# A fused attention and expert kernel on one core: one more chunk of unit 2's first product ahead of unit 1's second, eight g buffers for five, and a table of shifts on the planner's due times

## The chip, the cores and the metric

The kernel runs on one core of one Trainium2 chip, in one launch. The metric is the device time of that core in microseconds. The kernel before has a median of 1087.2 us over three runs (1081.66 to 1087.91).

## The reference, cut to what matters

```python
# attention with decay: 8 batches x 8 heads, 576 positions, head size 64, all float32
cum = np.cumsum(np.log(np.clip(f, 0.0001, 1.0)), axis=-1)
scores = q @ k.T / 8 + cum[:, None] - cum[None, :]      # causal
attn = exp(scores - rowmax) / (rowsum + 1e-9)
x = (attn @ v)          # -> 4608 tokens x 512, heads side by side
# expert
h = x @ w_in            # 512 -> 2048
g = h * np.cos(h)
out = g @ w_out         # 2048 -> 512
```

w_in and w_out arrive as float64.

## The kernel before, in words

**Work.** A batch has four pairs of heads, `n` = 0 to 31 in all. For each pair the kernel loads q and k with the running sums of log f, forms the scores in PSUM (TensorE, "PE"), takes the row extremum (VectorE, "DVE", L692 or L853), the exponential (ScalarE, "ACT", L702 or L858), turns the weights round, multiplies them with v (L729 or L908) and leaves x as two float16 halves `xh` and `xl`. The first four pairs go through `attention32` (plain float32, turned on PE at L655); the others go through `attention`, whose weights are turned by a DMA transpose (L884). Pairs 0 to 3 hold their q and k in the ring `g` (`load32`, L619 to L627).

**The expert** is cut in units: two per batch, of 320 and 256 tokens, numbered `u` = 0 to 15 in the code (unit 1 and unit 2 of the title are `u` = 0 and `u` = 1). `gemm1(u, c)` (L924) makes chunk c of four of the first product: four groups of twelve matmuls (L938), each group into one tile of the PSUM ring `hp` (three tiles), each tile copied by ACT into the SBUF ring `h` (three buffers, L944). Then follow, for the chunk as a whole, two DVE operations into `r` (one buffer, L953 and L955), ACT's sine (L957), DVE's product with h (L959), ACT's float16 copy (L966) and the remainder on DVE or POOL (L967 or L968); the last two write the ring `g`. `gemm2(u, m)` (L971) reads the four g buffers of a unit: 48 matmuls (L984) into one `hp` tile, ACT's scaled copy (L990), a store.

**Weights.** Both matrices are read as pairs of 32-bit words and put together by three DVE operations per tile (L483, L487, L491), squared on ACT for a bound (L502) and split in two float16 halves by ACT (L512) and DVE (L519). Raw tiles of w_in pass through the ring `h`, those of w_out through the ring `g`.

**What sets the order.** Nothing is issued while the code runs through its loops: `op` only records operations with a cost, an engine and a priority `prio`, and their dependences. Rings are handed out in that recording order: buffer k of a ring waits for all users of buffer k minus the ring's size, and the first operation on a ring's buffer comes behind the first operation on the buffer before it. So in the recording order of `moe(u)` chunk 0 of unit u, the four `gemm2` of unit u-1 and chunks 1 to 3 of unit u take the `hp` tiles, and PE keeps to that order. In the first stretch the ring `g` is handed to the q and k of pairs 0 to 3 and to the sixteen raw tiles of w_out by turns: the second head of pair 1 stands five places behind the first head of pair 1.

`order` then plans: `rank` gives due times, `forward` runs a list schedule on modelled engines (at each step an engine takes, of what is ready, the operation with the earliest due time; a change of ACT's function table counts as `SWITCH` = 6 us of lateness), `backward` gives new due times from the end, and a second `forward` gives the order in which every engine's instructions are written. `forward` may also move an operation to its second engine (`alt`), and where PE would be idle in the first 200 us it writes filler matmuls on a constant tile (`pads`, L1050). Each engine runs its list in the order written; SP issues all DMAs from one list.

Of the kernel before, what the change touches and what calls it, by code (L numbers as in the profile page):

```python
# [40 lines left out]
POOLW = ()  # L41
SLQ, SLW, SLG = 1.0, 50.0, 0.0
LEAD = 2.5
HOLDV, HOLDW, HOLDR, HOLDX = 0.0, 0.0, 25.0, 18.0
NHP = 3
N32, NQ = 4, 8
ROUNDS = 2
AHEAD = 15
FILL, PAD = 200, 448
SWITCH = 6.0  # L50
TWO_PI = 2.0 * np.pi
NEG = -8.0e9
BUFS = dict(xs=1, stage=2, v2=2, vv=2, pt3=3, pt2=2, xh0=8, xl0=8, xh1=8, xl1=8, h=3, r=1, g=5, ot=1,
            pa2=1, pa1=3, hp=3, dg=1)


class Buf:
# [77 lines left out]
class Plan:  # L135
# [5 lines left out]
    def ring(self, name, make):  # L141
        old = self.rings.setdefault(name, [])
        b = Buf(make)
        if len(old) >= BUFS[name]:
            b.wait = old[len(old) - BUFS[name]]
        b.prev, b.name = old[-1] if old else None, name
# [86 lines left out]
    def order(self):  # L233
        self.rank()
        base = [(o.eng, o.cost, o.fn) for o in self.ops]
        for k in range(ROUNDS):
            if k:
                self.backward(end)
            for o, x in zip(self.ops, base):
                o.eng, o.cost, o.fn = x  # L240
            out, end = self.forward()
        return out

    def forward(self):

        free, avail, future, out, ends = {}, {}, [], [], {}
        for o in self.ops:
            free.setdefault(o.eng, 0.0)
            avail.setdefault(o.eng, [])
            o.n, o.ready = len(o.deps), o.hold  # L250
            if not o.n:
                heapq.heappush(future, (o.hold, o.id, o))
        t, dma_free, table, span = 0.0, 0.0, None, 0.0
        free["PE"] = PE0
        pe, port = Clock(), dict.fromkeys(SHARED, 0.0)
        while len(out) < len(self.ops):
            while future and future[0][0] <= t + 1e-9:
                _, _, o = heapq.heappop(future)
                if o.alt:
                    def done(e, c):  # L260
                        return max(t, free[e]) + c + sum(x.cost for x in avail[e] if x.due - x.first <= o.due - o.first)

                    if done(o.alt[0], o.alt[1]) <= done(o.eng, o.cost) + o.alt[3]:
                        o.eng, o.cost, o.fn = o.alt[:3]
                avail[o.eng].append(o)
            nxt = []
            for e, q in avail.items():
                if q and free[e] <= t + 1e-9:
                    o = min(q, key=lambda x: (x.due - x.first + (SWITCH if x.table not in (None, table) else 0.0), x.id))
                    q.remove(o)  # L270
                    out.append(o)
                    o.t = t
                    end = t + o.cost
                    if e == "PE":
                        o.pads = 0
                        if o.fill and t < FILL:
                            a = max([free[e]] + [x.end + 0.25 for x in o.bank])
                            if t - a > PADG:
                                o.pads = pe.pad(a, t - PADE)
                        end = pe.run(t, o.cost, o.moving)  # L280
                    if o.port and e in port:
                        x = port[SHARED[e]]
                        both = min(o.cost, max(0.0, x - t))
                        end += both
                        if both:
                            free[SHARED[e]] += both
                            port[SHARED[e]] += both
                        port[e] = end
                    if o.table not in (None, table):
                        table = o.table  # L290
                        end += T_TABLE
                    free[e] = end
                    if e == "SP":
                        dma_free = max(dma_free, t + min(o.cost, 0.625) + T_DMA0) + o.size / (DMA_BW if t > 10.0 else 0.6 * DMA_BW)
                        end = dma_free
                        if o.cost > 1.0:
                            free[e] = max(t + o.cost, end - 0.925)
                    span = max(span, end)
                    ends[o.id] = o.end = end
                    for s in o.succ:  # L300
                        s.ready = max(s.ready, end + (T_DMA1 if e == "SP" else LAT[e, s.eng]))
                        s.n -= 1
                        if not s.n:
                            heapq.heappush(future, (s.ready, s.id, s))
                if q:
                    nxt.append(free[e])
            if future:
                nxt.append(future[0][0])
            assert nxt or len(out) == len(self.ops), "operations wait for one another"
            t = max(t, min(nxt, default=t))  # L310
        self.span = span
        return out, ends
# [27 lines left out]
def fox_moe_kernel(ctx: ExitStack, tc: tile.TileContext, qkT, vp, fT, w1, w2, out):  # L340
    nc = tc.nc
# [59 lines left out]
    def ring(name, shape, dt, space=pool, tag=None):  # L401
        tag = tag or name
        return pl_.ring(tag, lambda: space.tile(shape, dt, name=tag, bufs=BUFS[tag]))

# [519 lines left out]
    def gemm1(u, c, pr):  # L924
        b, half = divmod(u, NU)
        w_ = UW[half]
        inv, a1, b1, o1 = ms[b]
        h = ring("h", [P, 4, UM], F32)
        for k in range(4):
            fs = slice(k * P, k * P + P)  # L930
            hp = ring("hp", [P, 512], F32, psum)

            def mm(hp=hp, fs=fs):
                n = 0
                for cb in range(NC):
                    xh, xl = X[b * NP + cb][half]
                    for w, x in ((0, xh), (1, xh), (0, xl)):
                        T.matmul(hp.get()[:, 0:w_], WS_[1][:, at(1, 4 * c + cb), w, fs], x.get(), start=(n == 0), stop=(n == 11))  # L938
                        n += 1

            xs = [z for cb in range(NC) for z in X[b * NP + cb][half]]
            op("PE", 12 * c_mm(w_), mm, reads=[*xs, *(WB[1, at(1, 4 * c + i)].part(j) for i in range(4) for j in range(3))], writes=[hp], prio=pr,
               fill=lambda hp=hp: hp.get()[:, 0:PAD])
            op("ACT", c_act(w_, True), lambda hp=hp, k=k: A.activation(  # L944
                h.get()[:, k, 0:w_], hp.get()[:, 0:w_], AF.Copy, scale=float(2.0 ** -24)), reads=[hp], writes=[h.part(k)], prio=pr)
        r = ring("r", [P, 4, UM], F32)
        hk = [h.part(k) for k in range(4)]
        N = 4 * w_

        def fl(x):  # L950
            return x.get()[:, :, 0:w_]

        op("DVE", c_dve(N, True) + 0.055, lambda: V.tensor_scalar(fl(r).bitcast(I32), fl(h), a1.get()[:, c:c + 1], 0.25, op0=ALU.mult, op1=ALU.add),  # L953
           reads=[*hk, a1], writes=[r], prio=pr)
        op("DVE", c_dve(N) + 0.045, lambda: V.scalar_tensor_tensor(fl(r), fl(r).bitcast(I32), b1.get()[:, c:c + 1], fl(h), op0=ALU.mult, op1=ALU.add),  # L955
           reads=[*hk, b1], writes=[r], prio=pr)
        op("ACT", c_act(N, aps=2), lambda: A.activation(fl(r), fl(r), AF.Sin, scale=inv.get()[:, c:c + 1], bias=halfpi),  # L957
           reads=[inv], writes=[r], prio=pr, table="sin")
        op("DVE", c_dve(N), lambda: V.tensor_tensor(fl(h), fl(h), fl(r), op=ALU.mult), reads=[r], writes=hk, prio=pr)  # L959
        g = ring("g", [P, 2, 4, UM], F16)  # L960
        gh, gl = g.part(0), g.part(1)

        def gx(i):
            return g.get()[:, i, :, 0:w_]

        op("ACT", c_act(N), lambda: A.copy(gx(0), fl(h)), reads=hk, writes=[gh], prio=pr)  # L966
        op("DVE", c_dve(N), lambda: V.tensor_tensor(gx(1), fl(h), gx(0), op=ALU.subtract), reads=[*hk, gh], writes=[gl], prio=pr,  # L967
           alt=("POOL", 0.9 * c_pool(N), lambda: G.tensor_tensor(gx(1), fl(h), gx(0), op=ALU.subtract), SLG))  # L968
        GT.setdefault(u, []).append((gh, gl))
# [24 lines left out]

    def moe(u):
        base = (u + 1) * NP / NU + LEAD
        gemm1(u, 0, base)
        if u > 0:
            for m in range(4):
                gemm2(u - 1, m, base + 0.25 + 0.25 * m)  # L1000
        for c in range(1, 4):
            gemm1(u, c, base + 1.0 + 0.25 * c)

    cleared = []
# [2 lines left out]
    def adv(n):  # L1007
        if n == N32 and not cleared:
            cleared.append(clear_pads())
        if n < len(gens):  # L1010
            pl_.first = AHEAD
            next(gens[n], None)
# [68 lines left out]
```

## Time and profile before

| | kernel before |
|---|---|
| runs | 1081.66, 1087.91, 1087.2 us; median 1087.2 us |
| profiled execution, first to last instruction | 1083.4 us (no other time of it is given) |
| PE matmul busy | 1053.6 us, 97% |
| PE weight load busy | 843.5 us, 78% |
| DVE busy | 825.9 us, 76% |
| ACT busy | 847.0 us, 78% |
| POOL busy | 166.5 us, 15% |
| mean granted TensorE clock | 0.991 of full |

A matmul's end in the trace is modelled, and matmuls overlap, so a busy PE is not a PE at its peak; the spacing of matmul starts tells how fast they pass. "Idle before" is the time an engine stood still just before an instruction, and the name behind the arrow is what ended that. The granted clock is 1.00 at 2.4 GHz and 0.50 at 1.2 GHz.

### The profile page before, as it was taken

The numbers are of one execution on the slowest core, as the hardware profiler recorded it, in microseconds if no ns is written. First come the engines' busy times: TensorE is split into PE (matmuls) and PEld (weight loads), VectorE is DVE, ScalarE is ACT, GpSimd is POOL, SyncE is SP. The second block draws the span as 40 slices with busy tenths as digits, with TensorE's granted clock in tenths as the row PEclk, the third lists the DMA queues.
The fourth block names the chain that finished last, engine by engine and source line by source line (L and its number), as shares of the span: only waits on it lengthen the run. The fifth ranks groups of instructions, "written<-read, shape, count | busy, mean of one in ns | idle before, by whom it ended". The sixth has DMA issues, their size and how long they took to land.

```text
span 1083.4 us, 23496 instructions
## 1 busy us (share of the span) xinstructions
PE 1053.6 (97%) x8981; PEld 843.5 (78%) x8981; DVE 825.9 (76%) x1796; ACT 847.0 (78%) x1754; POOL 166.5 (15%) x271
## 2 busy tenths in 40 slices
PE   9999988999999999999999999999999999999998
PEld 4777765778777887778777887788778887788787
DVE  6889999677886969777886969778886868662613
ACT  4767899588897979798897979887888988662522
POOL 1000011121111321131221311211121222000000
PEclk9989998999999999999999999999999999999999
DMA  8864544667776576756776576755676564330000
GB/s 288 288 205 167 109 99 96 155 166 148 156 177 151 110 151 154 149 110 161 161 175 151 119 151 151 171 117 141 155 174 143 126 141 80 82 59 21 7 19 20
DMA packets 256279, 146.37 MB, mean 135 GB/s; under 512 B 223336, under 2 KB 231528, under 8 KB 256168
## 3 DMA queue, kind: packets, MB, share of 16 engines
q1 hardware_dynamic: 256168, 144.88, 56.5%
q8 instruction: 70, 1.15, 0.4%
q14 instruction: 41, 0.34, 0.1%
HBM read 72.11 MB, written 10.62 MB: 76 GB/s over the span
## 4 chain that ended last, share of the span: by engine, by line
PE 61%; ACT 9%; DMA 3%; DVE 2%; issue 1%; POOL 0%; SPq 0%; ACTq 0%; DVEq 0%; POOLq 0%
PE hp L984 26%; PE hp L938 23%; PE pa L908 5%; PE pa L841 3%; PE pa L842 3%; DMA pt<-PS 2%; ACT pa L858 2%; ACT PS L875 1%; ACT r L957 1%; ACT L858 1%; DMA out_dram<-ot 1%; DVE PS L879 1%; ACT L957 1%; ACT QK L782 1%; ACT h L944 1%
## 5 line engine op out<-in xcount | busy, mean ns | idle before, releaser
L938 PE MATMUL hp<-xh,W1s 128*128 128x256 f16 (+1 forms) x2048 | 381.0, 286 | 9.7 <-ACT h L944 9.5
L984 PE MATMUL hp<-g,W2s 128*128 128x256 f16 (+1 forms) x3072 | 389.7, 286 | 0.4 <-DVE W2s L519 0.4
L938 PEld LDWEIGHTS <-W1s 128*128 128x128 f16 x3072 | 296.3, 98 | 87.8 <-issue 11.4
L984 PEld LDWEIGHTS <-W2s 128*128 128x128 f16 x3072 | 296.2, 98 | 76.7 <-DVE W2s L519 0.7
L938 PE MATMUL hp<-xl,W1s 128*128 128x256 f16 (+1 forms) x1024 | 292.6, 286 | 0.0
L879 DVE SCALAR_TENSOR_TENSOR PS<-pa,ri,PS 128x576 f16<-128x576 f32 (+2 forms) x280 | 140.5, 543 | 26.8 <-ACT PS L875 26.3
L853 DVE CUSTOM_DVE_ANT_0 pa<-pa,mask 128x576 f32<-128x576 f32 (+2 forms) x280 | 131.6, 511 | 28.8 <-PE pa L842 27.5
L875 ACT ACTIVATE PS<-pa,ri 128x576 f16<-128x576 f32 (+2 forms) x280 | 134.7, 542 | 17.2 <-DVE ri L866 8.7
L858 ACT ACTIVATE pa<-pa,nb 128x576 f32<-128x576 f32 (+2 forms) x280 | 140.6, 503 | 9.1 <-DVE nb L853 7.6
L944 ACT ACTIVATE h<-hp 128x320 f32<-128x320 f32 (+1 forms) x256 | 101.5, 420 | 38.4 <-PE hp L938 38.1
L863 POOL TENSOR_SCALAR ri<-L 128x1 f32<-128x1 f32 (+1 forms) x168 | 59.8, 356 | 426.0 <-ACT pa L858 412.0
L959 DVE TENSOR_TENSOR h<-h,r 128x1280 f32<-128x1280 f32 (+1 forms) x64 | 87.7, 1371 | 41.0 <-ACT r L957 41.0
L967 DVE TENSOR_TENSOR g<-h,g 128x1280 f16<-128x1280 f32 (+1 forms) x61 | 85.3, 1398 | 18.6 <-ACT g L966 18.5
L957 ACT ACTIVATE r<-r,halfpi,m_inv 128x1280 f32<-128x1280 f32 (+1 forms) x64 | 86.2, 1347 | 16.8 <-DVE r L955 16.2
L787 POOL TENSOR_TENSOR QK<-stage,QK 64x576 fp32r<-64x576 f32 x45 | 71.8, 1597 | 173.0 <-issue 110.2
L955 DVE SCALAR_TENSOR_TENSOR r<-r,m_b,h 128x1280 f32<-128x1280 int32 (+1 forms) x64 | 93.9, 1468 | 0.8
L953 DVE TENSOR_SCALAR r<-h,m_a 128x1280 int32<-128x1280 f32 (+1 forms) x64 | 58.6, 916 | 46.8 <-ACT h L944 45.3
L841 PE MATMUL pa<-QK 128*128 128x288 f32 (+4 forms) x288 | 90.0, 329 | 1.4 <-DVE PS L879 1.4
L966 ACT CAST g<-h 128x1280 f16<-128x1280 f32 (+1 forms) x64 | 74.0, 1156 | 17.5 <-DVE h L959 17.1
L908 PE MATMUL pa<-pt,vv 128*64 128x256 f16 (+2 forms) x1512 | 79.9, 257 | 6.9 <-DMA pt<-PS 6.5
L908 PEld LDWEIGHTS <-vv 128*64 128x64 f16 x1512 | 70.3, 112 | 20.0 <-issue 17.8
L990 ACT ACTIVATE ot<-hp,m_o 128x320 f32<-128x320 f32 (+1 forms) x64 | 32.2, 503 | 66.7 <-PE hp L984 41.7
(118 smaller groups left out, 1195.4 us busy)
## 6 DMA issues: line engine op xcount, KB each, us to landing
stage<-in_dram SPq DMA_DIRECT2D x48, 576.0 KB
stage<-in_dram SPq DMA_DIRECT2D x32, 320.0 KB
v<-in_dram SPq DMA_DIRECT2D x32, 320.0 KB
g<-in_dram SPq DMA_DIRECT2D x16, 512.0 KB
h<-in_dram SPq DMA_DIRECT2D x16, 512.0 KB
QC<-QK SPq DMA_DIRECT2D x48, 144.0 KB
out_dram<-ot SPq DMA_DIRECT2D x32, 160.0 KB
out_dram<-ot SPq DMA_DIRECT2D x32, 128.0 KB
```

Source lines behind the costliest of these rows:

```text
L841: T.matmul(c, hi[:, 0, isl], hi[:, 1, d], start=True, stop=False)
L853: op("DVE", c_dve(w) + 0.008, lambda view=view, ib=ib, o=o, w=w, mk=mk, c=c: V.tensor_tensor_reduce(out=view(ib, o, w), in0=view(ib, o, w) ...
L858: op("ACT", c_act(w, True, 2), lambda view=view, ib=ib, o=o, w=w, c=c: A.activation(view(ib, o, w), view(ib, o, w), AF.Exp, bias=nb.get()[ ...
L875: op("ACT", c_act(w, True, 1), lambda view=view, ib=ib, o=o, w=w, c=c, out_=out_: A.activation(out_(0), view(ib, o, w), AF.Copy, scale=ri. ...
L879: op("DVE", c_dve(w) + 0.06, lambda view=view, ib=ib, o=o, w=w, c=c, out_=out_: V.scalar_tensor_tensor(out_(1), view(ib, o, w), ri.get()[: ...
L908: T.matmul(d, vv.get()[:, jb, hd, kv], m, start=first and x == 0, stop=last and x == 2)
L938: T.matmul(hp.get()[:, 0:w_], WS_[1][:, at(1, 4 * c + cb), w, fs], x.get(), start=(n == 0), stop=(n == 11))
L944: op("ACT", c_act(w_, True), lambda hp=hp, k=k: A.activation(h.get()[:, k, 0:w_], hp.get()[:, 0:w_], AF.Copy, scale=float(2.0 ** -24)), re ...
L955: op("DVE", c_dve(N) + 0.045, lambda: V.scalar_tensor_tensor(fl(r), fl(r).bitcast(I32), b1.get()[:, c:c + 1], fl(h), op0=ALU.mult, op1=ALU ...
L957: op("ACT", c_act(N, aps=2), lambda: A.activation(fl(r), fl(r), AF.Sin, scale=inv.get()[:, c:c + 1], bias=halfpi), reads=[inv], writes=[r] ...
L959: op("DVE", c_dve(N), lambda: V.tensor_tensor(fl(h), fl(h), fl(r), op=ALU.mult), reads=[r], writes=hk, prio=pr)
L984: T.matmul(po.get()[:, 0:w_], WS_[2][:, at(2, 4 * c + k), w, msl], gh.get()[:, i, k, 0:w_], start=(n == 0), stop=(n == 47))
```

## The change

- `moe`: for `u == 1`, chunks 0 and 1 of `gemm1` are recorded ahead of the four `gemm2` of unit 0, chunk 1 with a priority 0.02 behind chunk 0; chunks 2 and 3 follow as before. Other units keep chunk 0 alone in front.
- The ring `g` has eight buffers in place of five. The room is taken from the scratch that the program sets aside for dynamic DMAs, which is set to 1024.
- `HOLDX`, the planned time before which the v loads of the first pairs are not issued, is 25 in place of 18 us.
- `order` ends with one more pass. Operations are put in groups by source line and priority; an operation's due time becomes its own start in the plan so far plus the shift that the table `SHIFT` holds for its group (0 if there is none). Moves to a second engine are off in this pass, and a change of ACT's table costs nothing in the choice. The table has 1347 entries from -367.6 to 1282.1 us, half of them within 20 us of zero.

```diff
-HOLDV, HOLDW, HOLDR, HOLDX = 0.0, 0.0, 25.0, 18.0
+HOLDV, HOLDW, HOLDR, HOLDX = 0.0, 0.0, 25.0, 25.
...
+EARLY = 2
...
-BUFS = dict(xs=1, stage=2, v2=2, vv=2, pt3=3, pt2=2, xh0=8, xl0=8, xh1=8, xl1=8, h=3, r=1, g=5, ot=1,
+BUFS = dict(xs=1, stage=2, v2=2, vv=2, pt3=3, pt2=2, xh0=8, xl0=8, xh1=8, xl1=8, h=3, r=1, g=8, ot=1,
             pa2=1, pa1=3, hp=3, dg=1)
+
+SHIFT = {
+    0: 2.6, 1: 50.9, 2: -45.6, 6: -4.6, 8: 39.7, 9: -8.9, 11: 124.1, 12: 13.5, 14: -37.1, 24: 47.5, 25: 4.9, 26: 33.8, 27: 46.2,
...
+}
...
-        return out
-
-    def forward(self):
+        self.shift()
+        return self.forward(0.0)[0]
+
+    def shift(self):
+
+        group = {}
+        for o in self.ops:
+            k = group.setdefault((o.fn.__code__.co_firstlineno, o.prio), o.id)
+            o.due, o.alt = o.t + o.first + SHIFT.get(k, 0.0), None
+
+    def forward(self, switch=SWITCH):
...
-                    o = min(q, key=lambda x: (x.due - x.first + (SWITCH if x.table not in (None, table) else 0.0), x.id))
+                    o = min(q, key=lambda x: (x.due - x.first + (switch if x.table not in (None, table) else 0.0), x.id))
...
     def moe(u):
         base = (u + 1) * NP / NU + LEAD
-        gemm1(u, 0, base)
+        first = EARLY if u == 1 else 1
+        for c in range(first):
+            gemm1(u, c, base + 0.02 * c)
         if u > 0:
             for m in range(4):
                 gemm2(u - 1, m, base + 0.25 + 0.25 * m)
-        for c in range(1, 4):
+        for c in range(first, 4):
             gemm1(u, c, base + 1.0 + 0.25 * c)
...
-    nc = _bacc.Bacc("TRN2", target_bir_lowering=False, num_devices=1)
+    nc = _bacc.Bacc("TRN2", target_bir_lowering=False, num_devices=1, dynamic_dma_scratch_size=1024)
```

## Rows read from the trace of the kernel before

**Rows 1.** The page's first part: busy time, share of the span, instructions, by engine.
```profile
PE 1053.6 (97%) x8981; PEld 843.5 (78%) x8981; DVE 825.9 (76%) x1796; ACT 847.0 (78%) x1754; POOL 166.5 (15%) x271
```

**Rows 2.** Filler matmuls by form: line, operation, count, busy us, mean ns, idle before.
```profile
L1050 PE MATMUL pa<-mask,ones 128*128 128x448 bf16 x126 | 26.6, 373 | 2.3 <-POOL ones L363 2.3
...
L1050 PE MATMUL hp<-mask,ones 128*128 128x448 bf16 x38 | 8.8, 352 | 0.0
```

**Rows 3.** Busy time by stretch: bounds, length, five engines, granted clock, DMA share, GB/s.
```profile
21.00:118.00 97.00, 92.91 (x584) 73.30 (x583) 85.81 (x263) 70.88 (x209) 3.68 (x19) 0.95 0.68 212
...
152.80:184.00 31.20, 23.93 (x170) 17.31 (x169) 30.10 (x72) 30.63 (x61) 2.62 (x7) 0.84 0.43 91
184.00:945.00 761.00, 749.14 (x6715) 607.87 (x6714) 606.32 (x1301) 650.96 (x1310) 152.66 (x214) 1.00 0.64 144
```

**Rows 4.** PE's instructions in time, 158.7 to 176.5 us: start, length, instruction, [idle before].
```profile
166.09 1.93 PE L908 MATMUL pa<-pt,vv 128*64 128x64 f16 x23 [5.78 <-DMA pt<-PS]
167.94 4.00 PE L839 MATMUL pa<-stage 68*128 68x448 f32 x8
...
174.37 1.80 PE L984 MATMUL hp<-g,W2s 128*128 128x320 f16 x12
```

**Rows 5.** PE alone by stretch: bounds, length, busy, granted clock, DMA share, GB/s.
```profile
166.10:171.90 5.80, 5.80 (x33) 0.50 0.08 32
171.90:178.00 6.10, 6.10 (x55) 0.85 0.19 54
```

**Rows 6.** Chain of waits near the end: start, length, work.
```profile
1041.85 1.31 PE hp L938 x12
```

**Rows 7.** A 256-token chunk's own operations by form, columns as in group 2.
```profile
L944 ACT ACTIVATE h<-hp 128x256 f32<-128x256 f32 x128 | 46.0, 395 | 15.5 <-PE hp L938 15.4
L955 DVE SCALAR_TENSOR_TENSOR r<-r,m_b,h 128x1024 f32<-128x1024 int32 x32 | 44.6, 1394 | 0.5
...
L957 ACT ACTIVATE r<-r,halfpi,m_inv 128x1024 f32<-128x1024 f32 x32 | 39.7, 1240 | 8.4 <-DVE r L955 8.1
L959 DVE TENSOR_TENSOR h<-h,r 128x1024 f32<-128x1024 f32 x32 | 39.2, 1225 | 21.8 <-ACT r L957 21.8
L967 DVE TENSOR_TENSOR g<-h,g 128x1024 f16<-128x1024 f32 x29 | 37.7, 1301 | 10.8 <-ACT g L966 10.7
L966 ACT CAST g<-h 128x1024 f16<-128x1024 f32 x32 | 33.6, 1049 | 8.1 <-DVE h L959 8.1
...
L953 DVE TENSOR_SCALAR r<-h,m_a 128x1024 int32<-128x1024 f32 x32 | 26.5, 828 | 26.1 <-ACT h L944 25.2
```

**Rows 8.** DVE's instructions in time, columns as in group 4.
```profile
174.05 1.48 DVE L967 TENSOR_TENSOR g<-h,g 128x1280 f16<-128x1280 f32 x1
```

**Rows 9.** Who PE waited for from 184 us on: total us, times, longest us.
```profile
PE hp L938 <- ACT h L944: 9.5, 9, 1.6
```

**Rows 10.** ACT's instructions in time around one such wait, then PE's.
```profile
345.13 1.28 ACT L957 ACT_TABLE_LOAD   x1
...
347.69 1.28 ACT L858 ACT_TABLE_LOAD   x1
...
350.14 0.38 PE L938 MATMUL hp<-xh,W1s 128*128 128x256 f16 x2 [1.60 <-ACT h L944]
```

**Rows 11.** ACT's table loads ahead of a sine, columns as in group 2.
```profile
L957 ACT ACT_TABLE_LOAD x51 | 65.4, 1283 | 0.9
```

**Rows 12.** SP's and PE's instructions in time in the first stretch.
```profile
17.05 0.43 SPq L635 DMA_DIRECT2D v<-in_dram  x1
...
39.23 2.79 PE L729 MATMUL hp<-v,pt 128*128 128x64 f32 x24
...
44.34 0.59 SPq L625 DMA_DIRECT2D g<-in_dram  x1
...
51.95 3.66 PE L684 MATMUL pa<-g 68*128 68x288 f32 x12 [1.22 <-DMA g<-in_dram]
```

**Rows 13.** All engines by stretch, columns as in group 3.
```profile
50.00:68.00 18.00, 16.78 (x75) 12.94 (x74) 13.07 (x46) 12.01 (x39) 0.29 (x2) 0.72 0.85 257
```

121 rows, old and new, of the table SHIFT are left out of this document.

## The prediction

> **What bounds the kernel now.** I read the page's busy times first. PE is busy for 97% of the span, DVE and ACT for under 80% [rows 1], which looks like a kernel with only 29.8 us (1083.4 less 1053.6) left to win. The list of PE's work by form corrects that: 164 filler matmuls that compute nothing hold 35.4 us of the busy time [rows 2]. Idle and filler together are 65 us; part of it lies before the first data and can't be won.
>
> Next the table by stretch, to see where the 65 us lie and which engine rules there [rows 3]. From 21 to 118 us PE turns round the first four pairs and writes fillers in the gaps; DVE is busy for 85.8 of 97 us, for it also puts the weights together. From 152.8 to 184 us PE is busy for 23.9 of 31.2 us at a mean granted clock of 0.84, while DVE and ACT are full (30.1 and 30.6 us): unit 1's second product waits for the split of w_out and for unit 1's elementwise chain. From 184 us on PE is the bound at full clock, and ACT is at 86% (651 of 761 us). A microsecond of PE idling saved anywhere moves the end by a microsecond, as long as the DVE and ACT work stays covered.
>
> Then PE's own list in the worst stretch [rows 4]: it stands for 5.78 us ahead of the last 23 matmuls of a v product, for the DMA that turns its weights. When it starts again the granted clock is 0.50, that is 1.2 GHz, for 5.8 us, and 0.85 in the mean of the next 6.1 us [rows 5]; the idling came before the fall. The second product begins at 174.37 us.
>
> Last, whom PE waits for once it is the bound: nine times for ACT's copy out of PSUM, 9.5 us in all [rows 9]. One of them shows the pattern: ACT loads the sine's table, runs the sine, loads the exponential's table back (1.28 us each load), and the copy that PE needs stands behind that; PE waits 1.60 us [rows 10].
>
> **The change part by part**, against the profiled execution's span of 1083.4 us.
>
> *Chunk 1 of unit 2 ahead of the second product.* Moved on PE: four groups of twelve matmuls, 1.31 us a group [rows 6], 5.24 us. It no longer stands behind `gemm2` of unit 1 in the order of the `hp` tiles but in front, so it can fill the hole. No DMA moves with it. Its own later work is four copies (1.58 us), a sine (1.24) and a cast (1.05) on ACT, with two table loads (2.57) 6.4 us, and 0.83 + 1.39 + 1.23 + 1.30 = 4.75 us on DVE [rows 7, 10]; it lands among engines that are full there, and the scheduler can put it behind the w_out split. What is queued behind it: its h buffer is the one of unit 1's chunk 2 (three in the ring), whose last reader starts at 174.05 us [rows 8]. Until then three groups fit in the three PSUM tiles (3.9 us); the fourth, and all of `gemm2` behind it in the tile order, waits. I take 3.9 us. If PE does not stand still, the clock need not fall: the half-clock stretch costs 2.9 us and the next 0.9 us [rows 5], 3.8 us, of which I take half, 1.9. Together **-5.8 us**. Bounds: -9.0 (all four groups and all of the clock); +1.2, if the 6.4 us on ACT go in front of the w_out split and push the second product by that, less the 5.2 us filled.
>
> *Eight g buffers.* Eight buffers matter where five made something wait. In the long stretch g is not what PE waits for [rows 9]. In the first stretch the load for the second head of pair 1 takes the buffer of that pair's first head, and is issued at 44.34 us; PE waits for it until 51.95 us [rows 12], and from 50 to 68 us the mean granted clock is 0.72 [rows 13], a loss of 18 x 0.28 = 5.0 us. With eight it takes the buffer of a raw w_out tile that is done earlier. How much the chain to the first product then gains isn't shown by any row. At most it gains what DVE leaves idle up to 118 us, 97 - 85.8 = 11.2 us [rows 3]; at worst a load that moves forward pushes back a weight tile of 512 KB, which at 290 GB/s is 1.8 us. I take the clock loss, **-5.0 us**, the nearest row; bounds -11.2 and +1.8.
>
> *The shifts and the last pass.* Nothing is computed more or less; every list can come out otherwise. Where PE is the bound they can only remove or add waits. Removable are the 9.5 us of copies behind a sine [rows 9]; I take half, **-4.8 us**, since a copy put ahead of a sine delays that chunk's chain, which something else will want. Bounds 0 and -9.5; new waits are a rival below. In the first stretch the shifts work inside the 11.2 us already counted.
>
> *HOLDX and the scratch.* The v load at 17.05 us moves to about 25 us; its reader starts at 39.23 us [rows 12]. A wait needs 14 us more, so no loss; two such loads of 320 KB less in the early traffic free 2.2 us at best. I take 0, bounds 0 and -2.2. The scratch costs nothing: SP issues all DMAs.
>
> Sum: -5.8 - 5.0 - 4.8 = -15.6, a span of 1067.8 us. The median lies 3.8 us above the profiled span; with that, **1071.5 us**. All bounds together give -31.9 (1055.3) and +3.0 (1090.2).
>
> **The rivals.**
>
> *A wait takes the hole's place (within 1%).* For it: DVE and ACT are busy for 60.7 of 62.4 engine-us in the stretch of the hole [rows 3], so PE's early chunk moves no bound, and `gemm2` starts as much later as PE was filled; the pair's loads start sooner but DVE's queue stays as long. Against it: after 184 us DVE has a fifth of its time free, so deferred work finds room. Only the -4.8 and some change of clock remain, 1080 to 1088 us, say 1083. The case that the lists hardly change, because due times equal to the old starts bring the old order back, falls here too: half the shifts are under 20 us. Chance 0.25.
>
> *The copies fall behind the sines (slower).* The last pass charges nothing for a table change. There are 51 loads for 64 sines [rows 11, 7], so 13 sines share one; and each sine with its two loads is 1.28 + 1.24 + 1.28 = 3.8 us on ACT, as long as the three PSUM tiles last (3 x 1.31 = 3.9 us), so any operation more between them stalls PE, at up to 1.60 us [rows 10]. Place: every chunk of 256 tokens from 184 us on. It decides from 14 stalls more: with the first two terms kept (-10.8), 10.9 us of loss need (10.8 + 10.9) / 1.6 = 14. With 20 more stalls the time is 1087.2 - 10.8 + 32 = 1108 us. Against it: ACT has 110 us free after 184 us, and the due times come from a plan that had paid for the changes. Chance 0.13. The Trainium skill, "ScalarE: Activation LUTs", section "Table sets: the hidden batching unit", speaks against such a pass: activations should be batched by table set, all of one and then all of the next; and the section "What ACT_TABLE_LOAD costs" puts a change at about 2.66 us, 1.28 for the load and the rest for a drain. By that a sine would hold ACT for 6.6 us, 2.8 us longer, and this rival would come to about 1163 us (20 x 2.8 us more), an estimate from that page. Here the trace has the load at 1.28 us and no drain behind it (a sine starts as its load ends), so the rows decide.
>
> *All the holes close.* The first stretch takes back DVE's 11.2 us, the chunk and the clock 9.0, all nine copies 9.5: 1087.2 - 29.7 = 1057.5 us, or 1055 with the v loads. For it: a table of 1347 shifts reaches every wait. Against it: the stretches before 184 us have almost no DVE time to give. Chance 0.10.
>
> **How the numbers follow.** My forecast, 1062 to 1076 us around 1071.5, has 0.52; all holes closing 0.10; no difference 0.25; slower 0.13. A measurement of this kernel tells about 1% from no change, 10.9 us, so the bounds are 1076.3 and 1098.1 us. Faster is the forecast with the closing of all holes, 0.62; same 0.25; slower 0.13. The range: below it stands the sum of the best bounds, 1055, with some 0.07 outside; above it the sum of the worst, 1090, takes in the no-difference case and leaves the slower case out. 1055 to 1090 leaves out 0.2; the likeliest case's own range is 1062 to 1076.
>
> **What would show it.** Right: L938 matmuls of 256 columns where PE now stands at 160 to 166 us, a granted clock near 1.00 from 152.8 to 184 us, the second product no later than 174 us; fewer fillers after 21 us and the load of 44.34 us issued by 35; fewer than nine waits of L938 for L944, and about 50 loads at L957. Wrong: the second product later by as much as PE was filled; the same clock fall with other work in it; loads at L957 near 64 with more waits at L938. The forecast falls if PE's idle after 184 us grows, whatever the front does, or if the front's DVE time turns out to have been the whole bound.

## The result, and the profile after

The changed kernel takes **1073.1 us** in the median of 11 runs (1070.77 to 1078.29). The kernel before, run beside it on the same chip, takes 1081.66 us in the median of 11 runs (1079.44 to 1089.86); its 1087.2 us further up was the median of three. The ratio is **0.9913, 95% interval 0.9888 to 0.9938**; it is taken over all runs of both kernels, here and below, and is not the quotient of the two medians (0.9921). The profiled execution took 1073.1 us over a span of 1071.4 us, so 1.7 us lie outside the span.

A change of some 0.9% is not read from the totals: the span fell by 12.0 us, PE's busy time by only 3.5 us [rows 1]. The page's first part after:

```profile
PE 1050.1 (98%) x8975; PEld 841.6 (79%) x8975; DVE 819.7 (77%) x1801; ACT 832.2 (78%) x1739; POOL 155.3 (14%) x271
```

The fillers are still there, 158 in place of 164 [rows 2]; 34.5 us of the 1050.1 is theirs:

```profile
L1186 PE MATMUL pa<-mask,ones 128*128 128x448 bf16 x123 | 25.6, 367 | 2.9 <-POOL ones L497 2.3 <-ACT PS L836 0.6
...
L1186 PE MATMUL hp<-mask,ones 128*128 128x448 bf16 x35 | 8.9, 371 | 0.9 <-DVE pt L778 0.9
```

The stretches of [rows 3] after the change (bounds, length, PE, weight load, DVE, ACT, POOL busy, granted clock, DMA share, GB/s), with one more after 220 us:

```profile
21.00:118.00 97.00, 91.31 (x602) 72.40 (x602) 91.76 (x282) 72.28 (x209) 3.31 (x19) 0.98 0.74 221
...
152.80:184.00 31.20, 28.63 (x240) 21.57 (x238) 30.56 (x63) 30.77 (x61) 2.67 (x6) 1.00 0.49 114
184.00:220.00 36.00, 32.67 (x216) 23.03 (x215) 25.22 (x58) 23.60 (x52) 4.25 (x10) 0.81 0.61 142
220.00:945.00 725.00, 721.30 (x6507) 589.34 (x6505) 574.57 (x1245) 620.17 (x1258) 137.91 (x203) 1.00 0.66 143
```

From 152.8 to 184 us PE is busy for 28.6 us in place of 23.9, at full clock. But between 184 and 220 us the clock is 0.81, where it was 1.00 before; PE's own list shows what stands there (start, length, instruction, idle before):

```profile
165.44 0.39 PE L1072 MATMUL hp<-xh,W1s 128*128 128x256 f16 x2
...
166.75 3.42 PE L1118 MATMUL hp<-g,W2s 128*128 128x320 f16 x24
...
187.14 0.22 PE L1042 MATMUL pa<-pt,vv 128*64 128x64 f16 x1
189.66 1.92 PE L1042 MATMUL pa<-pt,vv 128*64 128x64 f16 x23 [2.30 <-DMA pt<-PS]
192.62 5.88 PE L973 MATMUL pa<-stage 68*128 68x448 f32 x12 [1.03 <-DMA stage<-in_dram]
```

The hole of [rows 4] has moved to the next v product, 27 us later, and is 2.3 + 1.0 us long in place of 5.78. When PE goes on the clock is at 0.50, as it was behind the old hole [rows 5]:

```profile
187.00:192.50 5.50, 2.28 (x26) 1.57 (x24) 5.50 (x8) 3.64 (x6) 0.30 (x2) 0.74 0.74 157
192.50:198.00 5.50, 5.38 (x12) 3.74 (x13) 3.03 (x8) 1.81 (x2) 0.00 (x0) 0.50 0.70 138
198.00:202.00 4.00, 4.00 (x16) 2.11 (x14) 3.46 (x9) 1.71 (x4) 0.00 (x0) 0.50 0.44 150
202.00:208.00 6.00, 6.00 (x47) 4.11 (x47) 2.55 (x8) 6.00 (x17) 3.19 (x5) 0.89 0.24 70
```

Here it stays there for some 14 us. In a second profiled execution of the same changed kernel it is some 10 us, as in the kernel before (0.51 from 163.4 to 173.8 us):

```profile
197.40:207.80 10.40, 8.64 (x24) 5.43 (x25) 7.11 (x17) 3.38 (x5) 0.00 (x0) 0.51 0.68 152
```

Whom PE waits for from 184 us to the end (total us, times, longest); this is the whole list, and the 9.5 us of [rows 9] have become 0.7:

```profile
PE pa L1042 <- DMA pt<-PS: 3.4, 2, 2.3
PE pa L975 <- DVE PS L1013: 1.5, 2, 1.1
PE pa L973 <- DMA stage<-in_dram: 1.0, 1, 1.0
PE hp L1072 <- ACT h L1078: 0.7, 2, 0.5
PE pa L1042 <- DVE xl L1050: 0.4, 1, 0.4
```

**PE's loss by stretch.** To add up idle, fillers and half clock I use one measure, here and in all that follows: the time from each matmul's start to the next one's, less the interval that this form of matmul keeps at full clock when nothing waits; a filler counts as loss altogether. It is worked out over all matmul records of one execution; the interval taken as normal is a choice, and with another choice the figures move by about 1 us. "Again" is the second profiled execution of the changed kernel.

| stretch, us | before | after | difference | predicted | after, again |
|---|---|---|---|---|---|
| 0 to 21 | 18.9 | 19.5 | +0.6 | | 19.2 |
| 21 to 118 | 26.3 | 21.9 | -4.4 | -5.0 | 28.1 |
| 118 to 220 | 14.0 | 14.6 | +0.6 | -5.8 | 14.3 |
| 220 to the end | 14.1 | 5.2 | -8.9 | -4.8 | 4.6 |
| all | 73.2 | 61.2 | -12.0 | -15.6 | 66.2 |

The last column matters as much as the others: the first 118 us differ by 6 us between two executions of one kernel, so the -4.4 is no result. The loss after 220 us is 4.6 to 5.5 us in all five executions of the changed order (two of it, three with small edits) and 14.1 in the one execution of the kernel before. Its -8.9 us is about the whole difference of the medians, 1081.66 - 1073.1 = 8.6 us.

### The profile page after: what moved, and what is told of

Same layout as the page of the kernel before. It is cut to its first block, busy times and chain, and to the rows that moved or that the text cites. A ratio compares the mean times of both kernels' runs of the same rounds, so it can differ in the third digit from the quotient of the medians.

```text
span 1071.4 us, 23498 instructions
## 1 busy us (share of the span) xinstructions
PE 1050.1 (98%) x8975; PEld 841.6 (79%) x8975; DVE 819.7 (77%) x1801; ACT 832.2 (78%) x1739; POOL 155.3 (14%) x271
## 5 line engine op out<-in xcount | busy, mean ns | idle before, releaser
L1072 PE MATMUL hp<-xh,W1s 128*128 128x256 f16 (+1 forms) x2048 | 380.4, 286 | 1.1 <-ACT h L1078 1.1
L1072 PEld LDWEIGHTS <-W1s 128*128 128x128 f16 x3072 | 295.9, 98 | 78.6 <-issue 1.7
L1072 PE MATMUL hp<-xl,W1s 128*128 128x256 f16 (+1 forms) x1024 | 292.6, 286 | 0.0
L992 ACT ACTIVATE pa<-pa,nb 128x576 f32<-128x576 f32 (+2 forms) x280 | 141.1, 506 | 19.8 <-DVE nb L987 18.6
L997 POOL TENSOR_SCALAR ri<-L 128x1 f32<-128x1 f32 (+1 forms) x168 | 46.8, 279 | 410.4 <-ACT pa L992 404.9
L921 POOL TENSOR_TENSOR QK<-stage,QK 64x576 fp32r<-64x576 f32 x46 | 77.3, 1680 | 170.5 <-issue 116.4
L1091 ACT ACTIVATE r<-r,halfpi,m_inv 128x1280 f32<-128x1280 f32 (+1 forms) x64 | 86.2, 1347 | 18.8 <-DVE r L1089 18.3
L1101 DVE TENSOR_TENSOR g<-h,g 128x1280 f16<-128x1280 f32 (+1 forms) x62 | 84.2, 1358 | 14.1 <-ACT g L1100 13.7
L1089 DVE SCALAR_TENSOR_TENSOR r<-r,m_b,h 128x1280 f32<-128x1280 int32 (+1 forms) x64 | 91.3, 1426 | 0.7
```

The lines of the kernel that those rows point to most:

```text
L992: op("ACT", c_act(w, True, 2), lambda view=view, ib=ib, o=o, w=w, c=c: A.activation(view(ib, o, w), view(ib, o, w), AF.Exp, bias=nb.get()[ ...
```

## The experiments

Theory: the gain comes from the table, which takes the copies away from behind the sines after 220 us; the early chunk moves a hole that the clock then makes dear. Rivals: the buffers and the early chunk bring it; or a pass without table costs does, whatever its shifts. A kernel's line numbers shift with its edit; L948 and L949 below are L1072 of the changed kernel. Time before is that of the same chip.

**The last pass taken out** (early chunk, buffers and HOLDX stay).

```diff
-        self.shift()
-        return self.forward(0.0)[0]
+        return out
```

> The changed kernel without its last planning pass and without the table: chunk 1 of unit 2 early, eight g buffers and HOLDX 25 stay. Theory (the table's shifts give the gain; the early chunk only moves the hole): nine or so waits of PE for ACT's copies, 8 to 11 us, are back after 220 us, and the time is 0 to 0.5% under the kernel before, ratio 0.995 to 1.002. Rival 1 (the early chunk and the buffers give the gain): ratio 0.989 to 0.994, as the changed kernel. Rival 2 (the last pass by itself gives it): as the theory here.

1083.92 us against 1086.86, ratio 0.9986 (0.9949 to 1.0023): no difference that shows. The loss is 12.8 us from 118 to 220 us and 13.8 after, and the copy waits are back, though with less than the 8 to 11 us expected:

```profile
PE hp L948 <- ACT h L954: 5.9, 6, 1.6
```

This run also shows the early chunk without the shifts. The hole is at the same v product as in the changed kernel and longer, 3.01 us for 2.30, and yet the clock stays at 1.00 from 118 to 220 us:

```profile
191.23 1.08 PE L918 MATMUL pa<-pt,vv 128*64 128x64 f16 x23 [3.01 <-DMA pt<-PS]
118.00:220.00 102.00, 92.27 (x733) 67.64 (x731) 93.39 (x219) 92.36 (x190) 12.18 (x26) 1.00 0.58 127
```

So the chunk can be early and the clock full, and the loss is 12.8 us all the same: besides the 3.0 us for the v product, PE waits there 4.2 us for copies and 1.9 us for the split of w_out. And a wait of a given length doesn't tell whether the clock falls.

**The pass kept, the table emptied.**

```diff
-SHIFT = {
...
-}
+SHIFT = {}
```

> The changed kernel with an empty table: the last pass runs with the plan's own starts as due times and no charge for a change of ACT's function table. Theory: the copy waits stay at 8 to 11 us after 220 us, ratio 0.995 to 1.003, within 0.3% of the run without the pass. Rival 2 (the pass by itself, without the charge, puts the copies ahead of the sines): copy waits under 3 us, ratio 0.989 to 0.993. Rival 1: ratio 0.989 to 0.994 with the copy waits still there.

1086.01 us, ratio 0.9997 (0.9965 to 1.0029), 17.1 us lost after 220 us, with the copy waits there again. The pass is worth nothing without its numbers.

```profile
PE hp L949 <- ACT h L955: 6.8, 7, 1.6
```

**Eight g buffers alone**, in the kernel before, with the scratch.

```diff
-... g=5, ot=1,
+... g=8, ot=1,
```

> The kernel before with eight g buffers (and the smaller scratch) and nothing else. Theory: the fourth q load can go earlier but DVE stays the front's bound, ratio 0.998 to 1.002. Rival (the third term of the prediction: the buffers are worth the clock loss of 50 to 68 us): 5 us less, ratio 0.994 to 0.997, with the mean granted clock of 50 to 68 us above 0.9.

1087.49 us, ratio 1.001 (0.9979 to 1.0042). The buffer of the load of [rows 12] is free far earlier: POOL clears it at 24.23 us, where it was 38.97 us before. But the load is issued at 42.69 us in place of 44.34, no more, and PE runs through 50 to 68 us at half clock. POOL's list, and the stretch:

```profile
24.23 0.15 POOL L624 MEMSET g<- 68x64 f32 x1 [18.72 <-PE pa L684]
```

```profile
50.00:68.00 18.00, 17.97 (x69) 15.84 (x70) 16.30 (x39) 9.32 (x26) 0.15 (x1) 0.50 0.90 280
```

Nor does it come forward with the pass taken out or the table emptied (46.4 and 46.5 us), and in the changed kernel it goes out at 49.08 us, later than before. The loads there at 17.51 and 21.00 us are those of pair 0's second and pair 1's first head, as at 17.52 and 19.55 us before.

```profile
49.08 0.59 SPq L759 DMA_DIRECT2D g<-in_dram  x1
```

**The early chunk taken out of the changed kernel**, with the table's entries renumbered for the operations that change places.

```diff
-EARLY = 2
+EARLY = 1
...
-            o.due, o.alt = o.t + o.first + SHIFT.get(k, 0.0), None
+            o.due, o.alt = o.t + o.first + SHIFT.get(k + 14 if 654 <= k < 678 else k - 24 if 678 <= k < 692 else k, 0.0), None
```

> The changed kernel with chunk 1 of unit 2 back behind the second product of unit 1 (the table's entries follow their groups). Theory: the early chunk moved the hole of 160 to 184 us to 187 to 207 us and closed nothing, so the time is that of the changed kernel within 0.3%, ratio 0.989 to 0.995, copy waits after 220 us under 3 us, and a hole with a fallen clock lies near 160 to 180 us again. Rival 1 (the early chunk is worth its 5 us): ratio 0.996 or more.

1134.33 us, ratio 1.0464 (1.04 to 1.0528), a miss for the theory, and far outside the 5 us that the rival spoke of, though its "0.996 or more" takes the number in. 45 us are lost after 220 us, in waits most of which neither kernel has and at a clock of 0.90 from 220 to 305 us. The first three rows of the list from 184 us on:

```profile
PE pa L975 <- DVE PS L1013: 6.7, 8, 1.8
PE hp L1072 <- ACT h L1078: 5.0, 5, 2.9
PE pa L1042 <- DVE vm L553: 4.8, 1, 4.8
```

It does not price the early chunk: the shifts are added to starts of a plan, and under another plan the same numbers put operations in other places. The chunk's price is better read without the table: from 118 to 220 us the loss is 14.0 us with one early chunk (g buffers alone) and 12.8 with two (pass taken out), one execution of each.

**One half of the table at a time**, cut at 205 us of the plan, once the later and once the earlier part.

```diff
-            o.due, o.alt = o.t + o.first + SHIFT.get(k, 0.0), None
+            o.due, o.alt = o.t + o.first + (SHIFT.get(k, 0.0) if o.t >= 205.0 else 0.0), None
```

> The changed kernel, but only those shifts of the table kept that belong to operations the plan starts at 205 us or later; the last pass itself, EARLY = 2 and the eight g buffers stay. Theory (the gain lies after 220 us, where the table takes away the waits of L1072 for the copies at L1078; the stretch before it gives about 4 us): PE's loss after 220 us 5 to 8 us against 14.1 before, at most three waits of L1072 for L1078, 1074 to 1079 us. Rival (the shifts are fitted to one plan from end to end, so a part of them is worth nothing or harms, as with the chunk taken out): loss after 220 us 13 us or more, 1083 us or more.

> The other half: only the shifts of operations that the plan starts before 205 us. Theory: the first product begins at 114 to 119 us as with the whole table, the copy waits after 220 us are back (six or more, loss after 220 us 12 to 15 us), 1079 to 1084 us. Rival 1 (the front holds the gain): 1076 us or less. Rival 2 (fitted from end to end): new waits after 220 us, loss above 16 us, 1088 us or more.

The later half alone: 1098.84 us against 1082.65, ratio 1.0129 (1.0074 to 1.0185), 29.7 us lost after 220 us. The earlier half alone: 1092.58 us, ratio 1.0081 (1.0055 to 1.0108), 23.8 us lost there. Both are slower than no table, so my theory's numbers fell in both, and the rival holds: the table is fitted from end to end. The earlier half is the sharper case. Up to 220 us it loses what the changed kernel loses (55.5 against 56.0 us), and from there on it lacks the later shifts; ten copies wait, and v products for their weights too (from 184 us on):

```profile
PE hp L1072 <- ACT h L1078: 7.9, 10, 1.6
PE pa L1042 <- DMA pt<-PS: 7.0, 4, 3.8
```

So behind the same 220 us the later shifts are worth 23.8 - 5.2 = 18.6 us in these executions; some 5 us of it are a clock of 0.66 from 350 to 365 us. That the 9.7 us above the kernel before (23.8 against 14.1) are the price of the state in which the front leaves the queues is a reading, not shown by a run. The later half alone, behind another front, has copies and the softmax at the head of the list:

```profile
PE hp L1072 <- ACT h L1078: 4.9, 5, 2.8
PE pa L975 <- DVE PS L1013: 4.8, 4, 2.2
PE pa L1042 <- DVE PS L1013: 4.6, 1, 4.6
```

**The copies moved by a rule**: in the kernel before, ACT's list was changed after 220 us so that 21 copies that were ready stand right behind the sine, ahead of the table's reload.

```diff
+        if s.table == "sin" and s.t > 205.0:
...
+                if act[j].size == 1 and all(d.end <= s.end + 0.3 for d in act[j].deps) and any(x.size != 1 for x in act[i + 1:j]):
...
+                    act.insert(k, act.pop(j))
```

> The kernel before, with 21 of ACT's copies out of PSUM after 220 us moved up on ACT's list, past exponentials or other work, to right behind the sine that they follow; all other engines keep their lists. Theory (the nine waits of 9.5 us are copies standing behind a table load and exponentials): copy waits 1 to 4 us, PE's loss after 220 us 6 to 9 us less, ratio 0.991 to 0.995. Rival (putting copies first makes the exponentials late and PE waits for those): copy waits down but other waits up by as much, ratio 0.998 or more.

1082.25 us against 1085.17, ratio 0.9983 (0.9953 to 1.0013). The rule does what it should, 9.5 us of copy waits become 2.1, but others grow; the loss after 220 us falls by some 2 us only (14.1 to 11.8). The first three rows from 184 us on:

```profile
PE pa L908 <- DVE xl L916: 2.6, 3, 1.2
PE hp L938 <- ACT h L944: 2.1, 4, 1.0
PE pa L841 <- DVE PS L879: 2.0, 3, 1.0
```

**The hole filled.** In the changed kernel, 12 fillers ahead of the v product of 187 us and 5 ahead of the scores behind it.

```diff
+    pes = [o for o in seq if o.eng == "PE"]
+    pv_, o = MARK[6, 0]
+    o.pads, o.fill = 12, lambda: pv_.get()[:, 0:PAD]
+    pes[pes.index(o) + 1].pads = 5
```

> The changed kernel unaltered, on the same chip as the three below, so that they can be set against it. Every theory: ratio 0.987 to 0.995 to the kernel before, a hole near 187 to 207 us with a granted clock near 0.5 in part of it.

> The changed kernel with twelve filler matmuls (0.19 us each at full clock) ahead of the v product that waits at 187 us and five ahead of the scores behind it; nothing else moves. Theory (the hole costs mostly by the half clock that follows PE's 2.3 and 1.0 us of idling): the granted clock from 187 to 208 us stays above 0.95, the scores and the second product there take 2.8 and 6.6 us for 5.7 and 9.1, and the time is 4 to 6 us under the changed kernel, ratio 0.982 to 0.990. Rival (the stretch is bound by what DVE and ACT deliver, so a faster PE waits for them a little later): clock high, time within 1.5 us of the changed kernel.

> The changed kernel with 17 filler matmuls in its hole at 187 to 193 us, once more, in five rounds, to narrow its interval. Theory (the granted clock's fall to 0.50 behind the hole costs 4 to 5 us less 3.5 us... of which the fillers' own 3.5 us lie in time in which PE stands anyway): 1068 to 1072 us, ratio 0.985 to 0.989, granted clock 1.00 from 187 to 220 us. Rival (the 1070.91 us of the first time was the spread of runs): 1073 us or more, ratio 0.991 or more.

The changed kernel again: 1073.54 us, ratio 0.9906 (0.9878 to 0.9933). The gain is there at equal clock too: of the runs in this set with a mean granted clock of 0.994, the six of the kernel before take 1079.14 to 1081.31 us, the one of the changed kernel 1074.1 us. With the fillers: 1070.91 us, ratio 0.9885 (0.9853 to 0.9917), and the second time 1068.99 us, ratio 0.9876 (0.9834 to 0.9919). That is 2.6 us under the changed kernel in the same set of runs, less than the 4 to 6 I expected of it; the intervals overlap, but both medians lie under every median of the changed kernel. The trace is clearer. PE's list of the filled kernel at the hole (L1191 are the fillers):

```profile
189.79 2.43 PE L1191 MATMUL pa<-mask,ones 128*128 128x448 bf16 x12
...
192.78 1.08 PE L1043 MATMUL pa<-pt,vv 128*64 128x64 f16 x23 [0.41 <-DMA pt<-PS]
193.80 1.12 PE L1191 MATMUL pa<-mask,ones 128*128 128x448 bf16 x5
195.47 3.05 PE L974 MATMUL pa<-stage 68*128 68x448 f32 x12 [0.55 <-DMA stage<-in_dram]
```

The same 23 matmuls take 1.08 us in place of 1.92, the same 12 take 3.05 in place of 5.88. The granted clock stays at 1.00 in both executions (rows of the first):

```profile
192.50:198.00 5.50, 4.67 (x39) 3.25 (x39) 5.37 (x11) 2.72 (x3) 0.00 (x0) 1.00 0.98 186
198.00:202.00 4.00, 4.00 (x30) 2.79 (x29) 3.77 (x13) 3.59 (x11) 0.27 (x1) 1.00 0.70 214
```

The loss from 118 to 220 us is 9.3 and 9.6 us, against 14.6 and 14.3 without fillers. The fillers' own 3.55 us are counted in that loss. This is the best version, faster than both kernels by its medians.

**The late small load moved.** In the changed kernel PE waits until 54.43 us for the loads of pair 1's second head, of which the small one, 18 KB, goes out at 48.41 us. The run was meant to bring that one forward to 21.0 us, where I took the head's 320 KB load to be.

```diff
+    o1, o2 = QLOAD[1, 1]
+    seq.remove(o2)
+    seq.insert(seq.index(o1) + 1, o2)
```

> The changed kernel with one small DMA (the 18 KB of running sums for the second head of pair 1, issued at 48.4 us) moved on SP's list to right behind that head's main load at 21.0 us. Theory (that small load is what holds PE at 48.7 to 54.3 us, but DVE, busy 91.8 of 97 us up to 118 us, is the front's bound): the scores start before 50 us and the first product comes 0 to 2 us earlier; time 0 to 2 us under the changed kernel. Rival (the load sets the front): first product 4 us or more earlier, time 4 us under, ratio 0.983 to 0.989.

The edit takes the two loads of that head by name and puts the small one behind the large one, and that shows where the large one is: at 49.08 us in the changed kernel, not at 21.0. SP's list of this run:

```profile
49.20 0.59 SPq L760 DMA_DIRECT2D g<-in_dram  x1
49.85 0.61 SPq L761 DMA_DIRECT2D g<-cum_d  x1
```

So nothing was brought forward, and the run decides nothing between its two theories. It serves as one more kernel in nearly the changed order: 1073.06 us, ratio 0.9924 (0.989 to 0.9959), 26.6 us lost from 21 to 118 us. PE's list there:

```profile
49.64 4.51 PE L1192 MATMUL pa<-mask,ones 128*128 128x448 bf16 x23
53.99 2.97 PE L820 MATMUL pa<-g 68*128 68x288 f32 x12
```

The 23 fillers are written into the order ahead of the scores, and the scores start where they end. What an earlier load of that head would be worth no run shows.

## Why the prediction was right, and where it was not

The time was right: faster, 1073.1 us against a forecast of 1071.5. Its sum was not right term by term.

**The early chunk, -5.8 us: the failing step.** Its first half is seen as written. L1072 matmuls stand at 160 us, the last group of twelve only at 165.44 with the second product right behind it, at 166.75 in place of 174.37, and from 152.8 to 184 us the clock is 1.00. The step that failed is that time filled there is time won: PE stands still again, at the next v product, and "if PE does not stand still, the clock need not fall" lacked its condition. DVE and ACT are as full as they were (30.6 and 30.8 of 31.2 us, [rows 3] with 30.1 and 30.6), and DVE writes that pair's last softmax until 186.6 us; the DMA that turns it lands when PE goes on, at 189.66 us, and PE had come sooner. That is the rival "a wait takes the hole's place", with a clock price that it did not put in us: the fillers give back 4.7 to 5.3 us of loss. But the clock isn't the whole of it: with the pass taken out it stays at 1.00 and the chunk still wins 1.2 us in place of 5.8, the rest going to other waits. The Trainium skill, "TensorE: Matmul & The Clock Gate", section "HAM oscillation — how this bites in real kernels", tells of the same pattern: a wait for a DMA, and the matmuls behind it at half clock. The trace agrees, with 0.50 from 192.5 to 202 us; with the pass taken out a wait of 3.01 us for the same DMA left it at 1.00.

**Eight g buffers, -5.0 us: the mechanism failed, and no gain is shown.** The step that failed is that the load waits for its buffer. With eight buffers the buffer is cleared 14.7 us earlier, and the load goes out 1.7 us earlier and the time stays where it was (1.001); in the changed kernel, where the forecast wanted the load out by 35 us, it is issued at 49.08 us. What holds it then is its place on SP's list, behind other loads and their waits: in the changed kernel SP stands 4.4 us for PE ahead of the v load of 48.03 us, the one just before. From 50 to 68 us the clock is indeed 0.91 in place of 0.72 [rows 13], though the load is later:

```profile
50.00:68.00 18.00, 16.93 (x91) 11.94 (x90) 15.32 (x51) 11.94 (x36) 0.38 (x3) 0.91 1.01 256
```

In the second execution, with the same order, it is 0.51 from 64 to 78 us. The two executions lose 21.9 and 28.1 us from 21 to 118 us. The term took its size from one stretch of one execution, in a part that differs by more than the term from execution to execution.

**The shifts, -4.8 us: right in its mechanism, too small.** It measured -8.9 us, and the copy waits fell by 8.8 us, from 9.5 to 0.7. Shown is that the table as a whole brings the gain, for without its numbers the gain is gone and the copies wait again; that the copies are all of it is the sum of the waits, not a run of its own. I took half of the 9.5 us, since "something else will want" the time; that is true of the local rule, which got back 2.3 us, and not of a table that places everything else as well. What ACT does now around the time of [rows 10]:

```profile
340.24 1.28 ACT L1091 ACT_TABLE_LOAD   x1
341.53 1.24 ACT L1091 ACTIVATE r<-r,halfpi,m_inv 128x1024 f32<-128x1024 f32 x1
342.68 0.64 ACT L1078 ACTIVATE h<-hp 128x256 f32<-128x256 f32 x2
...
348.98 1.24 ACT L1091 ACTIVATE r<-r,halfpi,m_inv 128x1024 f32<-128x1024 f32 x1
350.12 0.36 ACT L1078 ACTIVATE h<-hp 128x256 f32<-128x256 f32 x1
350.50 1.28 ACT L992 ACT_TABLE_LOAD   x1
```

The copies follow the sine at once, and a second sine runs 7 us later on the same table before the exponential's is loaded.

**The slower rival** (copies fall behind the sines) went the other way: fewer loads, not more, with 46 ahead of a sine where [rows 11] had 51:

```profile
L1091 ACT ACT_TABLE_LOAD x46 | 59.0, 1283 | 0.8
```

As in the trace before, a sine starts as its load ends, so the drain that the Trainium skill, "ScalarE: Activation LUTs", section "What ACT_TABLE_LOAD costs", adds is not seen here. Nor is the number of loads what decides: the slowest kernel of all, the one with the early chunk taken out, has 45 such loads.

**HOLDX, 0:** the v load goes out at 27.43 us, its reader starts at 37.30 without a wait; right.

**The frame.** The median was put 3.8 us above the span; it is 1.7 in this execution, and the 1087.2 us that this came from was 5.5 us above the median of 11 runs. The span was forecast at 1067.8 and came out at 1071.4. So errors met in a good number: a gain of 15.6 us forecast and 8.6 measured by the medians, with one term nearly twice too small and two that didn't show, against a starting time 5.5 us too high. That the time came within 1.6 us of the forecast is in part luck.

## What to carry to other kernels

Where PE is the bound, work pulled into a hole can move the hole to the next point where the full engines are late, as it did here with and without the shifts; follow the next product's inputs to that point before booking the gain, and try a few dummy matmuls in the new hole if the clock falls behind it (17 of them took 2.6 us off the median here). A table of due times is worth what it is only with the exact program it was fitted to: half of it, or one recording order changed, was slower than none. Take two executions before sizing a term from a stretch, for the spread of the start can be larger than the term.

## What the runs showed of the hardware that was not expected

- The same kernel's runs roughly follow its mean granted clock: of the 11 of the changed kernel, 1070.77 us ran at 0.995, 1074.87 at 0.992 and 1078.29 at 0.989.
- The same hole doesn't always meet the same clock. In the changed kernel PE had stood for 2.30 us when the clock fell, and the 23 matmuls behind that already ran at half clock (1.92 us); it stayed at 0.50 to 202 us although PE was busy throughout from 192.6. In the second execution the same 23, after 2.29 us, took 1.08 us, and the clock fell in the next wait, of 2.18 us. With the pass taken out PE stood for 3.01 us at full clock. With 17 fillers, 3.55 us of work, it stayed at 1.00 in both executions.
